# Infini-attention beside a Fourier mixer: the maxima's transpose in front of the transposed scores, and three small moves in the preparation

## The chip, the cores and the metric

The kernel runs on one core of a Trainium2 chip. The metric is the time of one execution on the device in microseconds (us), the median of several runs. The engines are called TensorE (PE in the profile, with PEld for its weight loads), VectorE (DVE), ScalarE (ACT), GpSimd (POOL) and SyncE (SP, which issues the DMAs). Each engine takes its instructions in the order in which the code lists them.

## What is computed

Two independent layers, side by side in the output (2048 rows, 576 + 576 columns, float32).

```python
# A: 32 heads of 18 features, 4 segments of 512 rows, with a memory M, z carried over the segments
logits = einsum("bhqd,bhkd->bhqk", qs, ks) * scale + mask   # mask: -1e9 for keys behind the query
p      = softmax(logits);  a_dot = p @ vs
a_mem  = (phi(qs) @ M) / (phi(qs) @ z + 1e-6)
o      = g * a_mem + (1 - g) * a_dot ;  M += phi(ks)^T vs ;  z += sum phi(ks)
out_A  = concat(o) @ wo
# B: real part of a 2-D DFT by matrices
a = x @ hid_re^T ;  b = x @ hid_im^T ;  y = seq_re @ a - seq_im @ b
```

In the reference the mask is added where `ar[:, None] < ar[None, :]`, so a query sees the keys up to its own place. A softmax may subtract any number near the maximum of a row, since it cancels.

## The kernel before

**Stages.** First (to some 218 us) the projections of A, segment by segment, with the memory and its lookup; q, k and v go to DRAM split into bfloat16 parts. Then one long loop, `attention()`, does the softmax part of A, with the matmuls of B (`dense()`) put between its slots. Last comes the output projection of A. The kernel is scheduled by hand: the order of the code is the order on every engine.

**The loop.** `attention()` runs over p = 0 to 67. A pass p begins work on a pair of heads, of which the even one (`even(...)`) and the odd one (`odd(...)`) go two different ways; `G` is a group of four heads, so two passes make a group. A pass is cut into eight slots by `yield SLOTS[i]`; at each one the main loop calls `tick()`, which runs what `later(n, ...)` has put off by n ticks, and then takes pieces of `dense()` until its share of the work is done. Lags say how many passes behind a step works: `F_LAG` 2, `T_LAG` 3, `V_LAG` 4.

**Scores of the even heads.** These are computed twice. `s_fill` (L753 and the helper `smallest`, L750) multiplies q and k (L744) and takes the row extremes with VectorE, only to know the maximum. `maxima(G)` (L791 to L797) packs the results of a group, on GpSimd, into a 128 x 128 bfloat16 tile `mb`, three parts to a number. `maxima_transpose(G, o)` (L799 to L805) turns that tile with one TensorE matmul (L801) into the columns 384 to 511 of a PSUM tile `o`, has ScalarE copy 24 partitions of it into `mt` (L803), and issues two DMAs, one tick later, that write `mt` into the rows 108 to 110 of the stacked queries `qs`. With these rows the transposed scores come out of the matmul with the maximum already subtracted.

**Transposed scores.** `t_fill` (L807 to L831) computes them three passes later, in three kinds, each into one bank of PSUM, the memory that TensorE writes (512 float32 columns a bank) that `bank("t", ...)` gives out in turn (two banks). Kind 0 is four matmuls of 128 columns (L818) and an exponential of 512 (L831). Kind 1 is one matmul of 384 columns (L821) and two exponentials of 384 (L830 and L831); the free last 128 columns of its bank take the transposed maxima of a group, where there is one. Kind 2 is L826 and L827. The group whose maxima are turned in pass p (p even) is G = p/2 - 1: for p = 4 to 64 within `t_fill` of kind 1, 31 times; for p = 2, where no `t_fill` runs yet, in a bank of its own, `trm`, right behind the first slot.

**Other PSUM banks.** `s` (two banks) holds the scores of `s_fill` and, of the odd heads, those of kinds 1 and 2 of `f_fill`; kind 0 of `f_fill` takes a `t` bank. `d` (three) holds the products of `dense()`; `pv` (one) the weighted values.

**Preparation.** The last segment's four blocks `project_v(3, j)` are followed by steps for the loop: `stacks` allots and presets `ks`, `c_cut(n)` splits the n-th chunk of B's input into a rounded upper part (ScalarE, L451 and L453) and the rest, its lower part (L456 and L458, one tick later, on the engine given, GpSimd where none is), and `attention_constants()` (L477 to L483) sets the mask `causal` and zeroes the two `mb` tiles.

Of the kernel before, what the change touches and what calls it, by code (L numbers as in the profile page):

```python
# [12 lines left out]
F32 = mybir.dt.float32  # L13
# [9 lines left out]
S, D, H, DH, NSEG, L = 2048, 576, 32, 18, 4, 512  # L23
P = 128
# [16 lines left out]
def infini_attention_and_fnet(ctx: ExitStack, tc: tile.TileContext, xT, wqk, w8, wv, wo, beta, xtT, cT, hT, out):  # L41
# [402 lines left out]
    def c_cut(n, engine=pool):  # L444
        if n < len(CHUNKS):
            raw = c_raw.pop(n)
            hi = sr.tile([P, 4, P], F32R, name="chi", bufs=3)
            lo = sr.tile([P, 4, P], F32R, name="clo", bufs=3)
            t = sr.tile([P, P], F32R, name="xtail", bufs=3) if CHUNKS[n][2] == 5 else None
            c_split[n] = hi, lo, t  # L450
            act.activation(hi, raw[:, :4], AF.Copy)  # L451
            if t is not None:
                act.activation(t, raw[:, 4], AF.Copy)  # L453

            def low():
                engine.tensor_tensor(lo, raw[:, :4], hi.bitcast(F32), OP.subtract)  # L456
                if t is not None:
                    engine.tensor_tensor(t[64:], raw[64:, 4], t[64:].bitcast(F32), OP.subtract)  # L458
            later(1, low)
# [17 lines left out]
    def attention_constants():  # L477
        t = CAUSAL[0]
        pool.memset(t, 0.0)
        pool.affine_select(t[:, 384:], t[:, 384:], pattern=[[-1, P]], base=0, channel_multiplier=1,  # L480
                           compare_op=OP.is_ge, fill=LOWEST)
        for m in MB:
            pool.memset(m, 0.0)  # L483

    NG = 32

# [13 lines left out]
    for s in range(NSEG):  # L500
        more = s < 3
        if s == 0:
            warm_up()
        open_qk(s)
        if s:
            memory()
        else:
            tick()
        for n, m in enumerate((0, 1, 2, 3, 8, 4, 5, 6, 7)):
            project_qk(s, m)  # L510
            tick()
            if not more and n in (5, 7):
                h_split(0, (n - 5) // 2)
            if s and n < (8 if more else 4):
                copy_parts(s - 1, 2 * n)
                copy_parts(s - 1, 2 * n + 1)
            if s in (1, 2) and n >= 4:
                load_x(s + 1, n - 4)
            if not more and n == 0:
                for k in range(5):  # L520
                    h_load(0, k)
            if not more and n == 4:
                p1k.close()
                sr = ctx.enter_context(tc.tile_pool(name="sb2r", bufs=1, side="right", reuse_waits="tile"))
                attention_tiles()
            if not more and n == 4:
                c_load(0)
                c_load(1)
                stacks(sr, 0)
                stack_load(0)  # L530
            if not more and n == 6:
                c_load(2)
        for j in range(4):
            project_v(s, j, lookup(s, j) if s else iter(()))
            tick()
            for k in ((0, 1), (2, 3), (4,), ())[j] if s == 0 else ():
                load_x(1, k)
            if more and j in (1, 2):
                split_x(s + 1, j - 1)
            if not more and j == 1:  # L540
                stacks(sr, 1)
            if not more and j == 2:
                attention_constants()
            if not more and j == 0:
                h_split(0, 2)
                h_split(0, 3)
            if not more and j == 1:
                h_split(0, 4)
                c_cut(0, dve)
                c_cut(1, dve)  # L550
            if not more and j in (1, 3):
                c_load(3 + j // 2)
            if more and j:
                accumulate(j - 1)
# [9 lines left out]
    def bank(name, shape, dtype, tag):  # L564
        turns[tag] ^= 1
        return ps.tile(shape, dtype, name=name, tag=f"{tag}{turns[tag]}", bufs=1)
# [232 lines left out]
    def maxima_transpose(G, o):  # L799
        t = o[:, 384:512]  # L800
        pe.matmul(t, MB[G % 2], ident16, start=True, stop=True)  # L801
        w = sa.tile([24, P], BF16, name="mt", bufs=2)
        act.activation(w, t[:24], AF.Copy)  # L803
        for h in range(2):
            later(1, dma, qs_bufs[G % 4][NPAIR:NPAIR + 3, 2 * h].rearrange("c (n t) -> c n t", n=4), w[12 * h:12 * h + 12])  # L805

    def t_fill(n, kind, maxima_of=None):  # L807
        G, h = divmod(n, 4)
        q, k = qs_bufs[G % 4][:NPAIR + 3, h], ks_bufs[G % 4][:NPAIR + 3, h]
        if kind == 0:  # L810
            PT[n] = (sa.tile([P, 1280], F16, name="phi", bufs=2), sa.tile([P, 1280], F16, name="plo", bufs=2),
                     sa.tile([P, 1280], F32, name="pf", bufs=3))
        hi, lo, f = PT[n]
        o = bank("t", [P, L], F32, "t")
        if kind == 0:
            for j in range(4):
                b = slice(j * P, (j + 1) * P)
                pe.matmul(o[:, b], k[:, b], q[:, b], start=True, stop=True)  # L818
            r, w = 0, 512
        elif kind == 1:  # L820
            pe.matmul(o[:, :384], k[:, :128], q[:, 128:], start=True, stop=True)  # L821
            if maxima_of is not None:
                maxima_transpose(maxima_of, o)
            r, w = 512, 384
        else:
            pe.matmul(o[:, 256:384], k[:, 256:384], q[:, 384:], start=True, stop=True)  # L826
            pe.matmul(o[:, :256], k[:, 128:256], q[:, 256:], start=True, stop=True)  # L827
            r, w = 896, 384
        if kind:
            act.activation(hi[:, r:r + w], o[:, :w], AF.Exp, bias=LIFT, scale=SCALE)  # L830
        act.activation(f[:, r:r + w], o[:, :w], AF.Exp, bias=LIFT, scale=SCALE)  # L831
# [89 lines left out]
    def attention():  # L921
        for p in range(NP + V_LAG):
            def even(lag, fn, *a):
                if 0 <= p - lag < NP:
                    fn(2 * (p - lag), *a)

            def odd(lag, fn, *a):
                if 0 <= p - lag < NP:
                    fn(2 * (p - lag) + 1, *a)

            if p < 2:
                stacks(sa, p + 2)
                OG.append(sa.tile([P, 4, 72], F32, name=f"og{p}"))
            if p == 0:
                value_load(0)
                stack_load(1)
            if p % 2 == 0:
                later(39, value_load, p // 2 + 1)
                later(30, memory_load, p // 2)
            if p == NP + 1:  # L940
                o_load(0)
                o_load(1)
            even(T_LAG + 1, t_lo, 0)
            odd(F_LAG + 1, f_exp, 2)
            odd(F_LAG + 1, f_split_hi)
            yield SLOTS[0]
            G = p // 2 - 1 if p % 2 == 0 and 0 < p <= NP else None
            even(0, s_fill, 0)
            even(T_LAG, t_fill, 0)
            even(T_LAG, t_fill, 1, G)  # L950
            if G is not None and p < T_LAG:
                maxima_transpose(G, bank("trm", [P, L], F32, "t"))
            odd(F_LAG + 1, f_split_lo, pool, 512, 1280)
            yield SLOTS[1]
            even(0, s_fill, 1)
            odd(F_LAG + 1, f_split_lo, dve, 0, 512)
            yield SLOTS[2]
            even(V_LAG, pv)
            even(0, s_fill, 2)
            even(T_LAG, t_mask)  # L960
            yield SLOTS[3]
            odd(F_LAG, f_fill, 1)
            even(T_LAG, t_fill, 2)
            odd(F_LAG, f_fill, 0)
            if p % 2 and p < NP:
                maxima(p // 2)
            yield SLOTS[4]
            odd(F_LAG + 1, f_turn)
            if p % 2:
                stack_load((p + 3) // 2)  # L970
                if p < 16:
                    later(2, copy_parts, 2, 8 + p // 2)
            elif 4 <= p < 36:
                later(2, copy_parts, 3, (p - 4) // 2)
            even(T_LAG, t_hi)
            yield SLOTS[5]
            odd(V_LAG, pv)
            odd(F_LAG, f_fill, 2)
            odd(F_LAG, f_exp, 1)
            even(T_LAG, t_lo, 1)  # L980
            even(T_LAG, t_lo, 2)
            yield SLOTS[6]
            odd(F_LAG, f_exp, 0)
            if p >= V_LAG:
                pv_out(p - V_LAG)
            yield SLOTS[7]
# [86 lines left out]
```

## Time and profile before

| | |
|---|---|
| Median of 3 runs | 997.3 us (997.13 to 998.15) |
| The profiled execution | 997.94 us |
| its span, first to last instruction | 996.2 us |
| granted TensorE clock | 0.999 of full speed |
| VectorE, ScalarE, GpSimd busy | 753.5, 712.0, 636.3 us |
| DMA | 208.92 MB, 210 GB/s |

How to read it: the profile is one execution, and its rows are single instructions or groups of them. A row of the timeline gives the start (us from the span's start), the duration, the engine, the line of the code, the operation, the tiles as out<-in with their shapes, and how many of a kind follow one another; in brackets stands how long the engine was idle before, and the instruction that ended the wait. A row of the waits gives who waited for whom, the total in us, how often, and the longest. A row of stretches gives, for each engine, the busy time and the number of instructions, then the clock, the DMA share and GB/s. A TensorE matmul's duration is longer than the distance to the next one, since matmuls overlap.

### The profile page before, as it was taken

How to read it: one execution, taken by the hardware profiler on the slowest of the kernel's cores; microseconds unless marked ns; L12 is line 12 of the kernel's file. 1: busy time of each engine (PE TensorE's matmuls, PEld its weight loads, DVE VectorE, ACT ScalarE, POOL GpSimd, SP SyncE). 2: the span in 40 equal slices, each digit the busy share in tenths (PEclk: the TensorE clock that was granted, in tenths of full speed). 3: DMA queues.
4: the chain of work that ended last, by engine and by line, in shares of the span. 5: the costliest groups of instructions: out<-in, count | busy, mean ns of one | idle time of the engine just before them, and what ended most of it. 6: DMA issues, size and time to landing. Idle time of an engine off the chain costs nothing.

```text
span 996.2 us, 25590 instructions
## 1 busy us (share of the span) xinstructions
PE 986.1 (99%) x9294; PEld 924.1 (93%) x9294; DVE 753.5 (76%) x2052; ACT 712.0 (71%) x1680; POOL 636.3 (64%) x700
## 2 busy tenths in 40 slices
PE   9999999999999999999999999999999999999998
PEld 8989989899999999999999999999999999999998
DVE  6657667594678777888898888888889899998321
ACT  7757575653887877878788888877777787777243
POOL 2657676675767677666766777766766767667000
PEclk9999999999999999999999999999999999999999
DMA  7537456767588898899999988779999999989455
GB/s 252 187 117 257 172 180 242 234 232 228 150 174 217 215 251 222 207 237 215 245 238 238 222 214 199 178 200 226 230 216 229 238 235 242 240 191 200 128 148 142
DMA packets 305615, 208.92 MB, mean 210 GB/s; under 512 B 206289, under 2 KB 260433, under 8 KB 305489
## 3 DMA queue, kind: packets, MB, share of 16 engines
q1 hardware_dynamic: 305248, 207.15, 80.8%
q8 instruction: 73, 1.20, 0.5%
q14 instruction: 54, 0.43, 0.2%
q10 hardware_dynamic: 240, 0.14, 0.0%
HBM read 121.32 MB, written 57.93 MB: 180 GB/s over the span
## 4 chain that ended last, share of the span: by engine, by line
PE 84%; DVE 6%; ACT 5%; issue 2%; DMA 2%; POOL 1%; SPq 0%; POOLq 0%; DVEq 0%; ACTq 0%
PE d L583 38%; PE s L744 7%; PE d L84 6%; PE v L84 4%; PE pv L862 4%; PE qk L250 4%; PE d L628 3%; PE d L629 3%; PE d L630 3%; PE pv L863 2%; PE m L363 1%; PE t L818 1%; PE qk L84 1%; DVE r L276 1%; PE t L821 1%
## 5 line engine op out<-in xcount | busy, mean ns | idle before, releaser
L750 DVE CUSTOM_DVE_ANT_0 s<-s,causal 128x128 f32<-128x128 f32 (+3 forms) x512 | 248.1, 504 | 94.0 <-PE s L744 84.8
L456 POOL TENSOR_TENSOR clo<-craw,chi 128x512 fp32r<-128x512 f32 x158 | 217.1, 1374 | 94.4 <-ACT chi L451 66.4
L583 PE MATMUL d<-wide,chi 128*128 128x288 f32 x1408 | 261.7, 303 | 0.0
L583 PEld LDWEIGHTS d<-wide,chi 128*128 128x128 f32 x1408 | 210.7, 188 | 2.7 <-issue 1.1
L583 PE MATMUL d<-wide,clo 128*128 128x288 f32 x704 | 173.3, 313 | 0.0
L784 POOL TENSOR_TENSOR hl<-pf,hl 128x768 f16<-128x768 f32 x64 | 112.6, 1759 | 69.3 <-ACT hl L780 58.7
L830 ACT ACTIVATE phi<-t 128x384 f16<-128x384 f32 x128 | 61.8, 483 | 103.8 <-PE t L827 103.8
L744 PE MATMUL s<-ks,qs 108*128 108x128 bf16 (+3 forms) x512 | 132.8, 303 | 2.7 <-DVE negm L750 2.1
L773 ACT ACTIVATE pf<-s,nb 128x128 f32<-128x128 f32 (+3 forms) x256 | 128.3, 527 | 6.2
L583 PE MATMUL d<-ab,chi 128*128 128x288 f32 x640 | 123.3, 302 | 0.0
L845 DVE TENSOR_TENSOR plo<-pf,phi 128x384 f16<-128x384 f32 (+1 forms) x128 | 122.9, 960 | 0.0
L583 PEld LDWEIGHTS d<-wide,clo 128*128 128x128 f32 x704 | 117.8, 189 | 1.9 <-issue 0.5
L451 ACT ACTIVATE chi<-craw 128x512 fp32r<-128x512 f32 x160 | 100.2, 627 | 6.1 <-DMA craw<-xtT 3.3
L831 ACT ACTIVATE pf<-t 128x384 f32<-128x384 f32 (+1 forms) x192 | 99.5, 518 | 5.9 <-PE t L818 5.5
L583 PEld LDWEIGHTS d<-ab,chi 128*128 128x128 f32 x640 | 97.8, 189 | 0.5
L780 ACT ACTIVATE hl<-pf 128x768 f16<-128x768 f32 (+1 forms) x128 | 87.4, 729 | 2.0
L583 PE MATMUL d<-ab,clo 128*128 128x288 f32 x320 | 83.0, 308 | 0.0
L628 PE MATMUL d<-wide,chi 128*128 128x288 f32 x256 | 81.3, 318 | 0.0
L629 PE MATMUL d<-wide,chi 128*128 128x288 f32 x256 | 75.7, 296 | 0.0
L630 PE MATMUL d<-wide,clo 128*128 128x288 f32 x256 | 75.6, 295 | 0.0
L845 POOL TENSOR_TENSOR plo<-pf,phi 128x384 f16<-128x384 f32 x64 | 61.4, 959 | 13.8 <-ACT pf L831 13.3
L784 DVE TENSOR_TENSOR hl<-pf,hl 128x512 f16<-128x512 f32 x64 | 69.4, 1084 | 0.1
(214 smaller groups left out, 2500.1 us busy)
## 6 DMA issues: line engine op xcount, KB each, us to landing
craw<-cT SPq DMA_DIRECT2D x128, 256.0 KB
ks<-kd SPq DMA_DIRECT2D x32, 432.0 KB
qs<-qd SPq DMA_DIRECT2D x32, 432.0 KB
craw<-xtT SPq DMA_DIRECT2D x32, 320.0 KB
vd<-vs SPq DMA_DIRECT2D x16, 440.0 KB
vst<-vd SPq DMA_DIRECT2D x32, 220.0 KB
qd<-p SPq DMA_DIRECT2D x16, 384.0 KB
kd<-p SPq DMA_DIRECT2D x16, 384.0 KB
```

The source lines that it names most:

```text
L84: pe.matmul(o, a, b, start=n == 0, stop=n == len(terms) - 1)
L451: act.activation(hi, raw[:, :4], AF.Copy)
L456: engine.tensor_tensor(lo, raw[:, :4], hi.bitcast(F32), OP.subtract)
L583: pe.matmul(o[h], a, b[:, h * 288:h * 288 + 288], start=start, stop=stop)
L628: pe.matmul(o, xh[:, k], wl[k][:, cs], start=k == 0, stop=False)
L629: pe.matmul(o, xh[:, k], wh[k][:, cs], start=False, stop=False)
L630: pe.matmul(o, xl[:, k], wh[k][:, cs], start=False, stop=False)
L744: pe.matmul(o[:, c:c + w], q[:, i * P:w], k[:, :w], start=True, stop=True)
L750: dve.tensor_tensor_reduce(o[:, c:c + w], o[:, c:c + w], CAUSAL[0][:, L - w:], scale=scale, scalar=-LOWEST, op0=OP.add, op1=OP.min, accum_ ...
L773: act.activation(f[:, FIRST_COL[i]:FIRST_COL[i] + w], o[:, c:c + w], AF.Exp, bias=nb[:, i:i + 1], scale=-1.0)
L784: engine.tensor_tensor(hl[:, 1, a:b], f[:, a:b], hl[:, 0, a:b], OP.subtract)
L845: (pool if kind == 2 else dve).tensor_tensor(lo[:, a:b], f[:, a:b], hi[:, a:b], OP.subtract)
```

## The change

Four edits. In `t_fill` of kind 1 the maxima's transpose, with ScalarE's copy, stands in front of the 384-column matmul. The transpose for the first group (p = 2, G = 0) moves from the first slot of the pass to behind the group of scores of the fourth, three slots later; it keeps a bank of its own, which now comes after that of `f_fill`. The lower part of the second chunk, `c_cut(1)`, is computed by GpSimd. `attention_constants()` runs after block 1 instead of block 2, behind the two `c_cut`, and VectorE zeroes the `mb` tiles.

```diff
         for m in MB:
-            pool.memset(m, 0.0)
+            dve.memset(m, 0.0)
...
-            if not more and j == 2:
-                attention_constants()
...
                 c_cut(0, dve)
-                c_cut(1, dve)
+                c_cut(1)
+                attention_constants()
...
         elif kind == 1:
-            pe.matmul(o[:, :384], k[:, :128], q[:, 128:], start=True, stop=True)
             if maxima_of is not None:
                 maxima_transpose(maxima_of, o)
+            pe.matmul(o[:, :384], k[:, :128], q[:, 128:], start=True, stop=True)
             r, w = 512, 384
...
             even(T_LAG, t_fill, 1, G)
-            if G is not None and p < T_LAG:
-                maxima_transpose(G, bank("trm", [P, L], F32, "t"))
...
             odd(F_LAG, f_fill, 0)
+            if p == 2:
+                maxima_transpose(0, bank("trm", [P, L], F32, "t"))
             if p % 2 and p < NP:
                 maxima(p // 2)
```

## The prediction, made before the changed kernel was run

> **What bounds the kernel now.** I read the page's first part first, then the waits of TensorE, then the busy time of the stretch that the attention loop fills.
>
> ```profile
> span 996.2 us, 25590 instructions
> PE 986.1 (99%) x9294; PEld 924.1 (93%) x9294; DVE 753.5 (76%) x2052; ACT 712.0 (71%) x1680; POOL 636.3 (64%) x700
> ```
>
> ```profile
> PE s L744 <- DVE negm L750: 2.1, 5, 0.8
> PE trm L801 <- POOL mb L797: 1.3, 1, 1.3
> ```
>
> ```profile
> 262.00:905.00 643.00, 641.34 (x6916) 603.16 (x6915) 548.95 (x1594) 507.30 (x1208) 455.48 (x498) 1.00 0.92 220
> ```
>
> TensorE (PE) is busy 99% of the span, and in the loop's 643 us it is busy 641.34. It takes its instructions in the order of the code, and next to nothing holds it: in the whole run it waited 2.1 us for VectorE's minima and 1.3 us for GpSimd's maxima. The other engines have a quarter to a third of their time free. So whatever shortens another engine's work is worth nothing, except where TensorE waits for it, and whatever makes TensorE wait is paid in full: no idle time lies behind it that could swallow it. I therefore ask of each edit one thing: which wait of TensorE does it take away, and which does it put in?
>
> **Part 1: the transpose of the maxima in front of the 384 columns (31 times).** Before, `t_fill` of kind 1 issues the 384-column matmul (L821), then the transpose of the maxima into columns 384 to 511 of the same PSUM tile (L801), then ScalarE's copy `mt` (L803), then ScalarE's exponentials of the 384 columns. After, the order on TensorE is transpose, 384 columns; and ScalarE's copy now stands in the program between the two. Here is one instance in the timeline (start, duration, engine):
>
> ```profile
> 350.07 0.39 PE L818 MATMUL t<-qs,ks 111*128 111x128 bf16 x4
> 350.30 0.33 PE L821 MATMUL t<-qs,ks 111*128 111x384 bf16 x1
> 350.46 0.22 PE L801 MATMUL t<-ident,mb 128*128 128x128 bf16 x1
> 350.49 0.77 PE L583 MATMUL d<-wide,chi 128*128 128x288 f32 x4
> 350.53 0.58 ACT L831 ACTIVATE pf<-t 128x512 f32<-128x512 f32 x1
> 351.01 0.25 ACT L803 ACTIVATE mt<-t 24x128 bf16<-24x128 f32 x1
> ```
>
> Before, TensorE goes on at once (L583 starts 0.03 us after the transpose) and ScalarE reads behind it. The whole question is whether the 384-column matmul, when it is issued behind the copy, has to wait for that copy. The two touch disjoint columns, so the data don't require it; but they share one bank of PSUM. Two places in the trace of before say how such a pair is ordered.
>
> ```profile
> ACT qe L218 <- DVE r L276: 14.4, 15, 1.7
> ```
>
> ```profile
> 121.61 0.69 DVE L276 TENSOR_TENSOR r<-qk,p 128x512 f32<-128x512 f32 x1 [0.26 <-ACT p L275]
> ...
> 122.33 0.60 ACT L218 ACTIVATE qe<-qk 128x512 f32<-128x512 f32 x1 [0.76 <-DVE r L276]
> ```
>
> ```profile
> 313.68 0.39 PE L744 MATMUL s<-ks,qs 108*128 108x128 bf16 x2
> ```
>
> ```profile
> 314.11 0.30 DVE L750 CUSTOM_DVE_ANT_0 s<-s,causal 128x128 f32<-128x128 f32 x1 [0.54 <-PE s L744]
> ```
>
> First, L276 and L218 only read the tile `qk` and write different tiles, yet ScalarE starts 0.03 us after VectorE ends (121.61 + 0.69 = 122.30), in all 15 places: even two readers of one bank are kept in program order. Second, the pair of L744 writes 128 columns and then 384 others; VectorE's first operation needs only the 128. A 128-column matmul takes 0.22 (the L801 row), so these were done at 313.90, and VectorE stood idle; it started at 314.11, 0.04 after the pair's end at 314.07. So disjoint columns of one bank are ordered too. I take it that the 384 columns will wait for the copy.
>
> [...]
>
> Now its price. In the new order the transpose takes the place of L821, and the 384 columns start when the copy has ended and TensorE has been woken. Waking takes 0.05 (fence of part 2: `mb` ends at 241.41, the transpose starts at 241.46), about what the transpose itself occupies; the two cancel. So a pause lasts from L821's old start to the end of `mt`. Nothing covers it, because TensorE works in order and the dense matmuls stand behind. In the instance above that is 351.26 - 350.30 = 0.96 us: the exponential of the 512 columns, 0.58, then the copy. ScalarE is free there; where it is behind, the pause is longer:
>
> ```profile
> 451.16 0.32 PE L821 MATMUL t<-qs,ks 111*128 111x384 bf16 x1
> ```
>
> ```profile
> 452.04 1.36 ACT L780 ACTIVATE hl<-pf 128x768 f16<-128x768 f32 x2
> 453.31 0.58 ACT L831 ACTIVATE pf<-t 128x512 f32<-128x512 f32 x1
> 453.79 0.25 ACT L803 ACTIVATE mt<-t 24x128 bf16<-24x128 f32 x1
> ```
>
> Here ScalarE still has the splits of L780 ahead of it, and the pause is 454.04 - 451.16 = 2.88 us. The first and the last of the 31, and the group's row:
>
> ```profile
> 263.39 0.33 PE L821 MATMUL t<-qs,ks 111*128 111x384 bf16 x1
> ```
>
> ```profile
> 265.93 0.25 ACT L803 ACTIVATE mt<-t 24x128 bf16<-24x128 f32 x1
> ```
>
> ```profile
> 894.31 0.33 PE L821 MATMUL t<-qs,ks 111*128 111x384 bf16 x1
> ```
>
> ```profile
> 896.25 0.25 ACT L803 ACTIVATE mt<-t 24x128 bf16<-24x128 f32 x1
> ```
>
> ```profile
> L803 ACT ACTIVATE mt<-t x31: 247/250/252, 265.9 to 896.2; 24x128 bf16<-24x128 f32 x31
> ```
>
> That is 2.79 and 2.19. Read pair by pair in the timeline, the 31 pauses go from 0.94 to 2.88 and sum to **46.3 us**. Do the pauses, by giving ScalarE time, shorten one another? They lie some 20 us apart, and in between ScalarE catches up with TensorE anyway:
>
> ```profile
> ACT phi L830 <- PE t L827: 103.8, 61, 3.1
> ```
>
> In 61 of the 64 passes it stood idle until TensorE's scores of kind 2 came, so its lag at the next copy is made afresh behind that point. I take off nothing for it and keep the floor, 31 x 0.94 = 29.1, as the lower bound. What waits behind: ScalarE's exponentials of the 384 columns come after its copy by a wake-up and a matmul (some 0.4 us), which its free time takes.
>
> **Part 2: the first maxima three slots later, and the preparation.** The rows of the beginning:
>
> ```profile
> 241.21 0.20 POOL L797 TENSOR_TENSOR mb<-negx,mb 128x8 bf16<-128x8 f32 x1
> ```
>
> ```profile
> 221.65 0.38 PE L744 MATMUL s<-ks,qs 108*128 108x128 bf16 x2 [0.31 <-DVE nd L407]
> 223.91 0.27 PE L744 MATMUL s<-ks,qs 108*128 108x256 bf16 x1 [0.83 <-DVE negm L750]
> ...
> 241.46 0.23 PE L801 MATMUL trm<-ident,mb 128*128 128x128 bf16 x1 [1.31 <-POOL mb L797]
> ...
> 245.55 0.80 PE L744 MATMUL s<-ks,qs 108*128 108x256 bf16 x4
> 253.73 0.39 PE L818 MATMUL t<-qs,ks 111*128 111x128 bf16 x4
> ```
>
> ```profile
> 218.55 1.64 DVE L456 TENSOR_TENSOR clo<-craw,chi 128x512 fp32r<-128x512 f32 x1
> 220.20 0.42 DVE L458 TENSOR_TENSOR xtail<-craw,xtail 64x128 fp32r<-64x128 f32 x1
> ```
>
> ```profile
> 223.31 1.16 POOL L417 TENSOR_TENSOR am<-nd,w 128x576 f32<-128x576 f32 x1 [2.53 <-ACT xtail L453]
> 226.79 1.28 POOL L456 TENSOR_TENSOR clo<-craw,chi 128x512 fp32r<-128x512 f32 x1
> 228.16 0.46 POOL L458 TENSOR_TENSOR xtail<-craw,xtail 64x128 fp32r<-64x128 f32 x1
> ```
>
> The transpose for G = 0 waited 1.31 us for `mb`. Moved behind the group of scores at 245.55 it is issued well after 241.41: **-1.31**. It keeps a tile of its own. With it move the copy and its two DMAs: SyncE's queue no longer stands at them, and the loads of `craw` behind them go first. The maxima are then written at about 246 and issued to land by 253.73, when the first transposed scores read them: some 7 us, against about 12 before. If that were too little, it is one wait of a few us, once; I cost it at nothing, with 0 to 2 as bounds.
>
> The lower half of the second chunk leaves VectorE (1.64 + 0.42 = 2.06) and goes to GpSimd (1.28 + 0.46 = 1.74). VectorE was late here: TensorE waited 0.31 and 0.83 for it. With 2.06 taken away, less two memsets of `mb`, both waits should go: **-1.14**. On GpSimd the new work lies in its idle 2.53 us ahead of 223.31, in the place that the mask's two instructions leave for an earlier block; without that cover it would hold the second chunk's first `clo` matmul, by 1.74 at most. The mask's own time is unchanged. The memsets I take as nothing on TensorE, since what they delay on VectorE is less than what leaves it.
>
> **The sum.** The later waits for `negm` (2.1 - 0.83 = 1.3) partly go, as VectorE gets 46 us of rest: -0.6, between 0 and -1.3. So 46.3 - 1.31 - 1.14 - 0.6 = +43.2. The profiled execution took 997.94 (its span, 996.2, and 1.7 around it), which is 0.64 above the median of the runs shown, 997.3. On that median the changed kernel takes 997.3 + 43.2 = 1040.5, say **1040.5 us**, 4.3% slower.
>
> **The rivals.** (A) Pauses at the floor: ScalarE is caught up at every copy, and each pause is 0.94. For it: ScalarE has 21% of the loop free (507.30 of 643.00). Against it: its lag comes from its order of work behind that idle time, not from a lack of time. 997.3 + 29.1 - 3.1 = 1023. (B) Pauses cost more than their length: TensorE loses its clock, or the late exponentials hold `pv`. Half the length on top gives 1040.5 + 23 = 1064. Against it: the granted clock stayed 1.00 in the loop and no pause is over 2.88. [...] (C) On the other side: the copy and the 384 columns are told apart by their columns, TensorE never waits, and only part 2 acts: 997.3 - 1.31 - 1.14 - 0.6 = 994.3, faster. It decides at the ordering alone: with no wait behind the copy the gain is about 3 us. For it: no row of before shows a matmul behind a reader of other columns of its bank. Against it: the two places in part 1. (D) No wait behind the copy, and the preparation gives nothing (the new GpSimd work takes back what VectorE frees): 997.3 - 1.3 = 996.0.
>
> **How the numbers follow.** Forecast 0.77, A 0.10, B 0.06, C 0.04, D 0.03. The forecast's own spread is some 8 us to each side (pauses that shorten one another by up to a sixth; 0.2 us more at each restart). The range for 8 in 10 reaches down to A and up to the forecast's end: 1023 to 1050. About 0.2%, or 2 us, is what a measurement here can tell from no change: slower 0.93, same 0.03 (D), faster 0.04 (C).
>
> **What would show it.** Right: the waits of TensorE have a new row, L821 waiting for ScalarE's `mt`, 31 times, some 30 to 45 us in total, with a longest near 2.9; the wait of `trm` for `mb` is gone, and those at 221.65 and 223.91 too; TensorE's busy time is unchanged and its share of the span falls to some 95%. Wrong: L821 starts right behind L801 while `mt` is still to come (C), or the row is there and sums to 29 or less (A), or matmuls behind a pause are longer than before (B).

## The result, and the profile after

The changed kernel takes **1045.34 us** (median of 5, 1039.71 to 1045.65) against 997.3 us before: a ratio of 1.0468, 95% interval 1.0441 to 1.0496. That is 48.0 us more; the forecast was 43.2 more (1040.5, range 1023 to 1050). The profiled execution took 1045.42, its span is 47.5 us longer than the one of before.

First the head of the page of the changed kernel, with the line of the granted clock:

```profile
span 1043.7 us, 25590 instructions
...
PE 996.1 (95%) x9294; PEld 932.8 (89%) x9294; DVE 751.2 (72%) x2052; ACT 716.5 (69%) x1680; POOL 634.8 (61%) x700
...
PEclk9999999999999999998999999999999999999999
```

The same 25590 instructions, the same work on VectorE, ScalarE and GpSimd to within 5 us, and TensorE's share down from 99% to 95%: no engine got more to do, one of them was kept waiting. TensorE's own busy time is 10 us longer, which will need an explanation: some 7.6 us are its clock (below), and up to 5.1 are the 31 transposes, whose 0.22 us, of which before all but some 0.055 lay under the next matmul, now stand open in front of a pause and count as busy; a little is given back elsewhere. All waits of TensorE in the changed kernel (who waits for whom, total us, times, longest):

```profile
PE t L822 <- ACT mt L802: 40.9, 31, 2.7
PE warm L239 <- DVE ones L68: 1.1, 1, 1.1
PE s L743 <- DVE negm L749: 0.4, 1, 0.4
PE kt L305 <- ACT kf L271: 0.4, 2, 0.2
```

The first row is new and is most of the story: 31 times the 384-column matmul, now L822, waits for ScalarE's copy `mt`. The rows of `trm` waiting for `mb` and of the scores waiting for `nd` are gone, and the one for `negm` shrank from 2.1 to 0.4. Here is the instance of the fifth group, the one that the prediction shows at 350 us, in the timeline of the changed kernel, TensorE first and then ScalarE:

```profile
359.68 0.39 PE L817 MATMUL t<-qs,ks 111*128 111x128 bf16 x4
359.91 0.22 PE L800 MATMUL t<-ident,mb 128*128 128x128 bf16 x1
360.92 0.32 PE L822 MATMUL t<-qs,ks 111*128 111x384 bf16 x1 [0.79 <-ACT mt L802]
360.94 0.83 PE L582 MATMUL d<-wide,chi 128*128 128x288 f32 x4
```

```profile
360.14 0.58 ACT L830 ACTIVATE pf<-t 128x512 f32<-128x512 f32 x1
360.62 0.25 ACT L802 ACTIVATE mt<-t 24x128 bf16<-24x128 f32 x1
361.28 0.49 ACT L829 ACTIVATE phi<-t 128x384 f16<-128x384 f32 x1 [0.41 <-PE t L822]
```

The transpose runs at 359.91, ScalarE does its exponential of 512 columns, then the copy, which ends at 360.87; TensorE starts the 384 columns 0.05 later, at 360.92. The row says 0.79, because the profile counts the wait from the modelled end of the transpose (0.22); from one start to the other 1.01 us passed, of which some 0.055 are the transpose's own (that much, 0.055 to 0.06, lies between the two starts where nothing holds the 384 columns, in the run of the copy behind). Where ScalarE is behind, in the first such place:

```profile
260.85 0.22 PE L800 MATMUL t<-ident,mb 128*128 128x128 bf16 x1
263.68 0.32 PE L822 MATMUL t<-qs,ks 111*128 111x384 bf16 x1 [2.61 <-ACT mt L802]
```

Read pair by pair, the 31 distances sum to 47.8 us, or 46.1 without the transposes' own time. The forecast, read from the trace of before, was 46.3, and it fits place by place: none of the 31 is off by more than 0.02 us.

### The profile page after: what moved, and what is told of

It is laid out like the page before. It is cut to its first block, busy times and chain, and to the rows that moved or that the text cites. A ratio compares the mean times of both kernels' runs of the same rounds, so it can differ in the third digit from the quotient of the medians.

```text
span 1043.7 us, 25590 instructions
## 1 busy us (share of the span) xinstructions
PE 996.1 (95%) x9294; PEld 932.8 (89%) x9294; DVE 751.2 (72%) x2052; ACT 716.5 (69%) x1680; POOL 634.8 (61%) x700
## 4 chain that ended last, share of the span: by engine, by line
PE 73%; ACT 13%; DVE 6%; issue 3%; POOL 2%; DMA 1%; SPq 0%; POOLq 0%; DVEq 0%; ACTq 0%
PE d L582 30%; PE s L743 6%; PE d L84 6%; PE v L84 4%; PE qk L250 4%; PE pv L861 4%; PE d L629 3%; PE d L628 3%; PE d L627 3%; ACT pf L772 3%; ACT hl L779 2%; PE pv L862 2%; ACT pf L830 2%; PE t L822 1%; PE m L363 1%
## 5 line engine op out<-in xcount | busy, mean ns | idle before, releaser
L582 PE MATMUL d<-wide,chi 128*128 128x288 f32 x1408 | 264.4, 305 | 0.0
L582 PEld LDWEIGHTS d<-wide,chi 128*128 128x128 f32 x1408 | 213.5, 190 | 11.0 <-issue 10.2
L582 PE MATMUL d<-wide,clo 128*128 128x288 f32 x704 | 175.5, 316 | 0.0
L627 PE MATMUL d<-wide,chi 128*128 128x288 f32 x256 | 82.7, 323 | 0.0
L629 PE MATMUL d<-wide,clo 128*128 128x288 f32 x256 | 76.8, 300 | 0.1
L628 PE MATMUL d<-wide,chi 128*128 128x288 f32 x256 | 76.7, 300 | 0.0
L783 DVE TENSOR_TENSOR hl<-pf,hl 128x512 f16<-128x512 f32 x64 | 66.1, 1032 | 0.1
```

The source lines that it names most:

```text
L582: pe.matmul(o[h], a, b[:, h * 288:h * 288 + 288], start=start, stop=stop)
L627: pe.matmul(o, xh[:, k], wl[k][:, cs], start=k == 0, stop=False)
L628: pe.matmul(o, xh[:, k], wh[k][:, cs], start=False, stop=False)
L629: pe.matmul(o, xl[:, k], wh[k][:, cs], start=False, stop=False)
L783: engine.tensor_tensor(hl[:, 1, a:b], f[:, a:b], hl[:, 0, a:b], OP.subtract)
```

## Experiments

**Is it the copy between the two matmuls?** My theory: TensorE waits for the copy that the program now lists between transpose and 384 columns, and the rest of the change helps a little. Rivals: part 2 costs too; or the order of the two matmuls itself costs.

The order undone (the rest of the change stays):

```diff
-            if maxima_of is not None:
-                maxima_transpose(maxima_of, o)
             pe.matmul(o[:, :384], k[:, :128], q[:, 128:], start=True, stop=True)
+            if maxima_of is not None:
+                maxima_transpose(maxima_of, o)
```

> The changed kernel with the 384-column matmul in front of the transpose again; the later first maxima and the preparation stay. Theory (TensorE waits for ScalarE's copy, and nothing else costs): all of the loss goes, and the two waits of part 2 stay away: 997.3 - 2.5 = 994.8, no row of the 384 columns waiting for mt, granted clock 0.999. Rival (part 2 also costs, through GpSimd's or SyncE's queue): above 997.3.

Measured: 995.77 against 997.15 us for the kernel before on the same chip, ratio 0.9985 (0.9976 to 0.9994). All of the loss is gone, and part 2 by itself is a small gain, 1.4 us instead of the 2.5 expected. Of its waits one is new, the price of the later first maxima that the prediction had bounded by 0 and 2:

```profile
PE s L743 <- DVE negm L749: 1.2, 4, 0.4
PE warm L239 <- DVE ones L68: 1.1, 1, 1.1
PE t L817 <- DMA qs<-mt: 0.4, 1, 0.4
```

The order alone (the kernel before, with the two statements exchanged, nothing else):

> The kernel before with the transpose in front of the 384 columns and nothing else changed. Theory: the 31 waits of about 46 us come, and the waits of TensorE for the first maxima and for VectorE in the preparation stay: 997.3 + 46 = 1043, or 1048 where the clock drops behind long pauses as it did in the changed kernel. Rival (much of the loss comes from part 2): below 1035.

Measured: 1048.49, ratio 1.0512 (1.0498 to 1.0527). In its profile the wait is the same, and those of the preparation are there again; the wait of `trm` for `mb`, which I had expected to stay, is not (why, see the parts of part 2):

```profile
PE t L823 <- ACT mt L803: 41.0, 31, 2.7
PE s L744 <- DVE negm L750: 1.2, 2, 0.8
...
PE s L744 <- DVE nd L407: 0.3, 1, 0.3
```

So the whole loss comes from this one exchange. The copy behind (transpose in front, as in the changed kernel; `maxima_copy` is the second half of `maxima_transpose`):

```diff
...
             if maxima_of is not None:
-                maxima_transpose(maxima_of, o)
+                pe.matmul(o[:, 384:512], MB[maxima_of % 2], ident16, start=True, stop=True)
             pe.matmul(o[:, :384], k[:, :128], q[:, 128:], start=True, stop=True)
+            if maxima_of is not None:
+                maxima_copy(maxima_of, o[:, 384:512])
```

> The changed kernel with the transpose still in front of the 384 columns on TensorE, but ScalarE's copy of it issued behind the 384 columns. Theory (the copy that stands between them costs): TensorE has nothing to wait for, 994.8, as with the order undone. Rival (the order of the two matmuls costs, or two writers of one bank): stays at 1040 to 1045.

Measured: **994.57**, ratio 0.9973 (0.9962 to 0.9984). TensorE's order is that of the changed kernel, and the loss is not there. All its waits, without a row for `mt`:

```profile
PE warm L239 <- DVE ones L68: 1.1, 1, 1.1
PE s L743 <- DVE negm L749: 1.1, 3, 0.4
PE kt L305 <- ACT kf L271: 0.4, 2, 0.2
```

It is not the transpose in front that costs, but a reader of the bank listed between two writers of it. This is also the best version of the study, faster than both kernels.

**What sets the length of a pause?** The transpose and its copy in front of kind 2 (L825 and L826 there), where ScalarE is mostly idle:

```diff
         elif kind == 1:
-            if maxima_of is not None:
-                maxima_transpose(maxima_of, o)
             pe.matmul(o[:, :384], k[:, :128], q[:, 128:], start=True, stop=True)
             r, w = 512, 384
         else:
+            if maxima_of is not None:
+                maxima_transpose(maxima_of, o)
...
-            even(T_LAG, t_fill, 1, G)
+            even(T_LAG, t_fill, 1)
...
-            even(T_LAG, t_fill, 2)
+            even(T_LAG, t_fill, 2, G)
```

> The changed kernel with the transpose and its copy in front of the two matmuls of kind 2 instead of the 384 columns of kind 1, 31 times as before; there ScalarE mostly stands idle and waits for TensorE. Theory (a pause is ScalarE's lag, then the copy, then the wake-up): the lag goes, and a pause is the transpose's 0.22, a start of 0.04, the copy's 0.25 and 0.05 for the wake-up, 0.56 us, less the 0.06 that the transpose takes anyway: 31 x 0.5 = 15.5 over 994.8, 1010, and no drop of the clock. Rival (a fixed price for each wait, 1.5 us): 1040.

Measured: 1011.05, ratio 1.014 (1.0124 to 1.0155). The same number of waits, each at the floor:

```profile
PE t L825 <- ACT mt L802: 11.0, 31, 0.4
```

31 pauses remain, 16.1 us in total from start to start without the transposes' own time, against 46.1. No price of its own for a wait shows here; it costs the time until the copy is done, and most of that was ScalarE's lag.

**What is the rest, 4.8 us over the forecast?** The granted clock of the changed kernel was 0.992 in the profiled execution, 0.999 before. In four of the five executions it was 0.991 or 0.992, and these took 1045.03 to 1045.65; in the fifth it was 0.998, and that one took 1039.71. To part clock from pause I split the 31 places into two sets of nearly equal total, the 10 longest pauses and the 21 others (`maxima_transpose` in front for the one set, behind the 384 columns for the other; the second kernel has `not in`):

```diff
+            front = maxima_of in (1, 2, 3, 10, 11, 14, 16, 17, 18, 31)
-            if maxima_of is not None:
+            if maxima_of is not None and front:
                 maxima_transpose(maxima_of, o)
             pe.matmul(o[:, :384], k[:, :128], q[:, 128:], start=True, stop=True)
+            if maxima_of is not None and not front:
+                maxima_transpose(maxima_of, o)
```

> The changed kernel with the transpose in front for only 10 of the 31 groups, those whose pauses were the longest there (1.95 to 2.93 us, G = 1, 2, 3, 10, 11, 14, 16, 17, 18, 31; from one start to the other they sum to 23.75 us, 23.2 without the transpose's own 0.055 each). Theory (pauses, and behind the long ones a clock at half speed for 3.41 us): 994.8 + 23.2 + 0 to 6 = 1018 to 1024, with a granted clock below 0.999 in some executions, and then the longer time. Rival (each restart costs a fixed 0.15 us beside the pause, and the clock nothing): 994.8 + 23.2 + 1.5 = 1019.5 in all of them.

> The other 21 groups, whose pauses were 0.99 to 1.78 us (they sum to 24.05, 22.9 without the transpose itself): as much pause as in the run of the long ones, in twice as many pieces. Theory: no drop of the clock, 994.8 + 22.9 = 1017.7 in every execution, granted clock 0.998 or 0.999. Rival (fixed price of 0.15 us for each restart): 994.8 + 22.9 + 3.2 = 1020.9, more than the long ones.

Measured: long 1026.46 (1021.66 to 1031.05), ratio 1.0284 (1.0257 to 1.0311); short 1015.09 (1014.65 to 1015.81), ratio 1.0171 (1.0158 to 1.0185). In the two profiles the pauses sum to 23.2 and 22.9 us, and the waits read:

```profile
PE t L823 <- ACT mt L802: 21.5, 10, 2.7
```

```profile
PE t L823 <- ACT mt L802: 19.4, 21, 1.6
```

Equal pauses, and yet the ten long ones cost 11 us more than the 21 short ones. The rival, a fixed price for each restart, says the opposite and falls. The granted clock of the long ones' five executions was 0.985 (1031.05 us), 0.990, 0.990, 0.991 (1025.6 to 1027.2) and 0.997 (1021.66); that of the short ones 0.999 or 1.000 in all. My numbers missed on both sides by 2.5 us: I had allowed 0 to 6 us for the clock, and there were six drops of the clock to half speed in the profiled execution, some 1.5 us each; and the short pauses were worth 2 us less than their length (below).

**The parts of part 2.** The first maxima's later place alone, and the preparation alone, each put into the kernel before as the diff of the change has it:

> The kernel before with the first maxima's transpose three slots later, nothing else. Theory: the wait of trm for mb goes and nothing takes its place: 997.3 - 1.3 = 996.0. Rival (the wait only moves, to the next thing that TensorE needs from GpSimd or from the maxima's DMAs): 997.3.

Measured: 996.95 against 997.78, ratio 0.999 (0.9981 to 1.0). Too little to be told from nothing with certainty, and 0.5 us less than the 1.3 expected.

> The kernel before with the preparation alone changed (second chunk's lower half by GpSimd, mask a block sooner, mb zeroed by VectorE). Theory: the two waits of TensorE at 221.65 and 223.91 go, 997.3 - 1.1 = 996.2, while the wait of trm for mb (1.31) stays. Rival (given back: TensorE comes sooner to the wait for mb, which grows by as much): 997.3, with trm waiting 2.4.

Measured: 995.98 against 997.78, ratio 0.9984 (0.9976 to 0.9993). That is more than the two waits, and in its profile `trm`, in its old place, doesn't wait at all; the waits are

```profile
PE s L743 <- DVE negm L749: 1.2, 4, 0.4
PE warm L239 <- DVE ones L68: 1.1, 1, 1.1
PE kt L305 <- ACT kf L271: 0.2, 1, 0.2
```

So the 1.31 us that I had taken from the one profile is not a fixed sum. `mb` was late there because the chunk's upper half on ScalarE had waited 3.10 us for a load of `craw`, and GpSimd, which takes the lower half before it packs `mb`, waited for that; in the profile of the preparation alone that wait is 0.91, in those of the other kernels between 0.95 and 3.54. To see whether the later place is needed once the preparation is changed, the copy behind with the first transpose in its early place again:

> As the copy behind, with the first maxima's transpose back in its early place (behind the first slot of p = 2), the preparation as changed. Theory (the preparation alone brings the maxima forward by more than their lateness of 1.31 us, so that the later place gains nothing): the same as the copy behind within 0.5 us, no wait of trm for mb. Rival (the first place costs 1.3 us whatever the preparation does): 1.3 us more, with a row of trm waiting.

Measured: 994.96, ratio 0.9976 (0.9965 to 0.9987); the version with the later place, beside it, 994.77. The medians agree with the theory. But the profiled execution, 996.45, has the wait,

```profile
PE trm L800 <- POOL mb L796: 1.1, 1, 1.1
```

while eight of the twelve took 994.09 to 994.99. With the transpose in its early place the wait of ScalarE for the load was 3.10 and 2.90 us in the two profiles in which `trm` waits (before, this run), and 1.46 and 0.91 in the two in which it doesn't (the order alone, the preparation alone). So the wait comes and goes with the landing of the load, and the later place only takes it away where it comes; for the executions without a profile this is inferred from their times.

**Does the order of the two matmuls do anything?** The copy behind and the order undone differ in it alone, and in the first runs they were 1.2 us apart. Once more, side by side:

> The kernel with the transpose in front and its copy behind the 384 columns, once more, beside the one with the order undone on the same chip. Theory of a hidden weight load (a 384-column matmul last hides more of the next float32 weight load than a 128-column one; 0.03 us or so in each of 31 places): about 1 us under the order undone, 994.6 against 995.7 at a before of 997.2. Rival (they are the same kernel as far as TensorE goes, and the first runs differed by chance): equal within 0.5 us.

> The order undone, once more, for the comparison with the copy behind. Theory: 1 us over it, some 1.5 us under the kernel before. Rival: the same as it.

Measured: 994.77 (994.43 to 995.09) against 995.71 (994.88 to 996.59, and one execution of 3526 us that stands alone), ratios 0.9969 (0.9956 to 0.9983) and 0.998 (0.997 to 0.9989). Again about 1 us. In the timelines of the fifth group, the copy behind against the rows of before that the prediction shows:

```profile
347.53 0.39 PE L820 MATMUL t<-qs,ks 111*128 111x128 bf16 x4
347.76 0.22 PE L824 MATMUL t<-ident,mb 128*128 128x128 bf16 x1
347.82 0.33 PE L825 MATMUL t<-qs,ks 111*128 111x384 bf16 x1
347.85 0.84 PE L582 MATMUL d<-wide,chi 128*128 128x288 f32 x4
348.52 0.30 PE L582 MATMUL d<-wide,clo 128*128 128x288 f32 x1
```

From kind 0 (347.53) to the first `clo` matmul (348.52) it is 0.99 us. Before it is 351.10 - 350.07 = 1.03, by the row

```profile
351.10 0.43 PE L583 MATMUL d<-wide,clo 128*128 128x288 f32 x2
```

Over the 31 places the stretch from the last matmul of kind 0 to the fourth one behind it (at 28 of them the second dense one) sums to 14.21 us before and 12.77 with the copy behind, 1.4 us less. The hidden weight load of my theory is not shown by any run; shown are the 1.4 us.

## Why the prediction was right, point by point

**The wait, and what sets it.** Right. The two signs in the trace of before, readers of one bank kept in order and disjoint columns of it too, did carry over to a matmul behind a reader: the new row has 31 waits, 40.9 us. (The 0.03 us that I gave for all 15 places of the first sign holds in six; in the other nine it is 0.09. ScalarE is behind VectorE in all.) Bank and tile are the same thing in this kernel; which of the two the order goes by, the runs don't tell.

**Its size.** 46.3 forecast, 46.1 found. That pauses don't shorten one another was right, and so was reading them from the old L821 to the end of the old `mt`: each of the 31 came out within 0.02 us of its forecast. Against this, the new order of the matmuls gives back 1.3 us (the stretch from kind 0 to the second dense matmul, counted as above, grew by 44.8 us in all, not 46.1), which I had not seen.

**Part 2.** -2.45 forecast. In the profile of the changed kernel the three waits are gone, and with the copy behind the 65th matmul of the scores (L744) starts 2.5 us sooner than in the profile of before. But I read one execution: 1.14 of it is steady, 1.31 comes and goes with the landing of a load. By the medians part 2 is worth 1.4 to 1.7 us (order undone). The later `negm` waits gave 0.9 by the rows of the waits, where I had put 0.6, and more from start to start (below).

**The step that failed: the clock.** I gave a loss of the clock 0.06, as a price of half the pauses. It came, at a third of that price: five drops to half speed, after five of the longest pauses. With the copy behind as the measure, place by place, each of the five puts the changed kernel back by 1.5 us beyond its pauses: some 7.6 us. (A drop lasts 3.41 us in the trace, at a clock of 0.50; by my estimate from these two that costs 1.7 at most.) Against such a loss I had set the clock of 1.00 in the loop of before and the longest pause, 2.88 us, and stopped there; but the loop of before had no such pauses (its longest wait was 0.4 us), and that 2.88 us are too short to lose the clock was my estimate, which no run had shown. The pauses were as long as I said, and the clock was lost on pauses of 2.16 to 2.93 us, from one start to the other. The two signs that go with this step came out against me: TensorE's busy time was not unchanged (996.1 us against 986.1), and matmuls behind a pause were longer, as I had written for B (15 of them took 3.48 us instead of 1.96, last section).

**The whole.** Some of the time is given back in the loop, at six matmuls in front of which TensorE stood in the profile of before and not in that of the changed kernel. The largest, before and after:

```profile
669.93 0.18 PE L863 MATMUL pv<-vst,plo 128*128 128x37 bf16 x1
670.48 0.27 PE L744 MATMUL s<-ks,qs 108*128 108x256 bf16 x1 [0.38 <-DVE negm L750]
```

```profile
705.50 0.18 PE L862 MATMUL pv<-vst,plo 128*128 128x37 bf16 x1
705.52 0.27 PE L743 MATMUL s<-ks,qs 108*128 108x256 bf16 x1
```

From one start to the next it was 0.55 us before and is 0.02 to 0.03 now. Three such places are waits for `negm` (0.9 us in the rows of the waits, 1.3 from start to start); what held the other three, which give 0.7, the rows don't say. In the profiles, then: 44.8 + 7.6 - 2.45 - 2.0 = 48.0, against 47.5 measured. The short pauses alone show the same: behind by 18.4 us at 836 us where their pauses sum to 19.5.

The forecast of 43.2 came nearer than its terms: without the clock these give 44.8 - 2.45 - 2.0 = 40.3, an estimate of some 1038 us. Two terms that I had missed or put too small, 1.3 and 1.4 us, stood against the clock that I had left out. That the one execution at a clock of 0.998 took 1039.71, within 1 us of the forecast, is in part luck.

**The rivals.** A fell: ScalarE's lag did come again, pause by pause. B, the clock, was real, at a third of the price that I gave it. C and D fell with the row of 31 waits.

## What to carry to other kernels

Before exchanging two statements that write disjoint parts of one PSUM bank, look for a reader listed between them: here the later writer waited for it, and for what stood ahead of it in the reader's queue, 0.99 to 2.93 us from one start to the other in each of the 31 places, though no data pass. Put the reader behind both writers: here the exchange then cost nothing (994.57 us against 995.77 with the old order). On an engine that is busy 99%, price such a wait as the time from the old start to the reader's end, instance by instance (46.3 us forecast so, 46.1 found); and ask of every pause of nearly 2 us or more what the clock will do (here all 16 steps of 3.41 us with 1.94 us or more of pause were followed by one at half the clock).

## What the hardware showed that was not expected

In the changed kernel the clock was lost on pauses of 2.16 to 2.93 us, and where they fell decided. Three stretches of the changed kernel, around the first pause (from, to; us; busy us and instructions of PE, PEld, DVE, ACT, POOL; granted clock; DMA):

```profile
261.44:264.85 3.41, 1.18 (x9) 1.17 (x9) 0.71 (x3) 2.97 (x7) 2.14 (x3) 1.00 0.92 296
264.85:268.26 3.41, 3.41 (x17) 3.26 (x16) 0.00 (x0) 1.19 (x4) 0.65 (x1) 0.50 0.68 221
268.26:271.68 3.42, 3.42 (x44) 3.23 (x44) 3.04 (x12) 1.28 (x3) 2.22 (x3) 1.00 0.11 29
```

In the first stretch TensorE was idle for 2.2 of 3.41 us; in the next the clock is half (0.50), and the 15 matmuls that start in it take 3.48 us, for which the copy behind took 1.96; then it is whole again (1.00). Up to the end of the work the drops are five; they begin at 264.85, 292.16, 469.65, 493.55 and 940.69 us, whole multiples (8, 60, 67, 198) of 3.413 us behind the first (675.84 us / 198): in this profile the drops lie on one grid of 3.413 us, each in the step behind one with a long pause. And a pause of 2.32 us that lay across a mark of the grid, from 315.63 to 317.95, was followed by no drop:

```profile
312.64:316.05 3.41, 3.21 (x27) 2.90 (x26) 3.23 (x9) 2.69 (x7) 2.03 (x2) 1.00 0.94 214
316.05:319.47 3.42, 1.52 (x12) 1.45 (x12) 1.28 (x5) 3.01 (x8) 2.38 (x3) 1.00 0.82 269
319.47:322.88 3.41, 3.41 (x44) 3.15 (x43) 1.74 (x8) 0.61 (x2) 1.55 (x1) 1.00 0.69 198
```

I laid the grid over the pauses of three profiles, the changed kernel, the order alone and the long pauses, and took from each pause (from 0.055 us behind the transpose's start to the 384 columns) its longest part within one step. All 16 steps with 1.94 us or more of pause are followed by a drop (five of them in the changed kernel, with 2.10 to 2.77; in the order alone, two of the drops last two steps), none of those with 1.90 or less (10 of them between 1.70 and 1.90). The border is less sharp than these two numbers: by the profile's busy time, in which the whole 0.22 of the transpose counts, two of the drops follow 1.83 and 1.84 us of idle time (in the order alone), while the step at 316.05 above, with 1.90, has none. So in these runs the border lies at 1.8 to 1.95 us, a step idle for a little over half. The five executions of the long pauses took 1021.66 to 1031.05 us, at mean clocks of 0.997 to 0.985. That the pauses fall differently on the grid from one execution to the next is my guess at the cause of this spread; with one profile a kernel it is not shown.
